# Attention with expert layers: batch 0 walked by halves of the sequence, its expert layers run as two groups of 256 tokens

## The chip, the cores and the metric

The kernel runs on one core of a Trainium2 chip. The time is device microseconds of one execution. The kernel before took 851.01 us (median of three runs, 849.23 to 852.69).

A core has five engines with queues of their own: TensorE (PE in the profile, with PEld for its weight loads), VectorE (DVE), ScalarE (ACT), GpSimd (POOL) and SyncE (SP), which here issues all transfers. Each works through its own instructions in order, and semaphores hold an instruction until what it needs is there.

## The reference, cut to what matters

Windowed attention with global tokens, for 8 batches and 8 heads of width 64. Each batch has 512 local and 32 global tokens. A global query sees all 544 keys. A local query sees the 32 global keys and the local ones at most 32 positions away. The 544 tokens of a batch, with their 8 heads side by side (512 columns), then go through an expert layer:

```
h = np.maximum(np.maximum(x @ w1, x @ w2), x @ w3)      # [512, 768] each
out = h @ w_out                                         # [768, 512]
```

The weights come as 64-bit floats, the rest as 32-bit floats.

## The kernel before, in words

**Tiles and steps.** Heads are taken in pairs, four pairs to a batch, 32 pairs (p) in all. The queries of a pair are cut into four tiles (t) of 128, so there are 128 steps (`sl`, with p and t from `divmod(sl, 4)`), 16 to a batch. The main loop of `body` (L510) walks these steps. In step `sl` it transposes the probabilities of the next step (`trans`, L338), computes scores and softmax some steps ahead (`next_scores`, `scores`, L300), multiplies probabilities with values (`pv`, L377), takes a part of the next pair's global queries (`glob`, `glob_soft`), transposes a part of the global probabilities (`transg`, L360), and prepares and loads what later steps need.

**Precision.** The first 26 to 28 steps multiply in full 32-bit floats. Later steps, and all expert matmuls, work in the faster rounded format (F32R) with each operand split into a high and a low part (`copy`, then `sub`), three matmuls to a product (high by high, high by low, low by high).

**Probabilities.** For steps 0 to 15 (`EARLY`) `scores` leaves them where the transposition reads them (`early`, one of five buffers in turn). From step 16 on they go by a transfer from `s` to `prob` (L334), a transfer being the way in which a tile gets into the rounded format without a computing engine. The global probabilities are scaled as a whole by `times`, and six transfers (L298) put their parts where `transg` reads them (`probg`).

**The expert layer.** `moe_group` (L415) is a generator that gives out one matmul at a time. For each of 6 x 3 blocks of 128 hidden columns it has 12 matmuls (L425) into one PSUM bank; copies and maxima over w1, w2 and w3 follow, and the split of h. Then come 18 matmuls for each 128 tokens (L444) with the output weights. `fill(n)` takes n matmuls from the generator. In the main loop 4 + 4 + 3 + 7 = 18 of them stand between the parts of a step. Batch b's 288 matmuls so fill the 16 steps of batch b + 1. Batch 7's and the global tokens' come at the end. In steps 0 to 15 there is no expert work.

**Weights.** `pieces` gives 24 pieces of 128 x 512 (18 of w1, w2 and w3, then 6 of w_out). `convert` takes one through five stages: the load of the 64-bit numbers into a staging tile (L160), an absolute value on ScalarE (L165), four integer operations on VectorE that put a 32-bit float together (L168 to L171), the high part on ScalarE (L178), the low part on POOL (L182). `weight_step` moves every piece under way on by one stage, takes one more into work and loads another. The list `WS` (L472) gives the number of such steps after each attention step: 13 through step 15, 17 in steps 16 to 25. Staging uses tiles that the expert layer later needs for h (`h0` to `h5`, six at first, fewer as the pieces go on); the scratch tile `cut` has six buffers.

**What sets the order.** Where an operation may run on several engines, a planner at build time (`least`, L79) takes the engine on which its own sums, with assumed costs, come out lowest. The framework adds all semaphores and buffer waits. It orders the instructions of each engine, the program's order being the priority. An explicit edge (`issue_after`, L349) puts everything that TensorE gets after the transposition of step 16 behind that transposition.

## Time and profile before

| | |
|---|---|
| Median of three runs | 851.01 us |
| The profiled execution's own time | 852.36 us |
| Its span | 850.6 us |
| TensorE busy | 811.6 us (95%) |
| VectorE busy | 566.0 us (67%) |
| ScalarE busy | 527.9 us (62%) |
| POOL busy | 510.0 us (60%) |
| First expert matmul | 76.6 us from the start |
| First expert matmul of batch 1 | 194.2 us from the start |

The profile shows one execution. Busy time is a union over an engine's instructions, and the span is what lies between the first and the last of them. A row of a window view gives the stretch, then the busy time of PE, PEld, DVE, ACT and POOL in it, the TensorE clock that was granted (1 is full), the busy share of the transfer engines and the rate in GB/s. A row of a group gives line, engine, operation, output and inputs, the count, and behind the bar the busy time, the mean duration in ns and the idle time of the engine before those instructions with what ended it. A row of waits reads: who waited, on what, us in total, how often, the longest.

### The profile page before, as it was taken

What the parts mean: (1) busy time and instruction counts of PE and PEld (TensorE: products, weight loads), DVE (VectorE), ACT (ScalarE), POOL (GpSimd) and SP (SyncE); (2) the same over time, 40 slices, a digit from 0 to 9 for tenths busy, and PEclk for the clock granted to TensorE, in tenths of its full rate; (3) what the DMA queues carried; (4) which work ended last, traced back from release to release, by engine and by line L of the source; (5) the groups of instructions that cost most, each with busy time, mean ns of one, the idle gap of its engine ahead of it and who ended that gap; (6) DMA issues with size and microseconds to landing.
All of it is one profiled execution on the core that took longest, in us unless ns stands there. A gap on an engine that the chain in (4) does not pass through costs nothing.

```text
span 850.6 us, 15712 instructions
## 1 busy us (share of the span) xinstructions
PE 811.6 (95%) x4452; PEld 674.6 (79%) x4452; DVE 566.0 (67%) x1784; ACT 527.9 (62%) x1479; POOL 510.0 (60%) x683
## 2 busy tenths in 40 slices
PE   6767987999999999999999999999999999999997
PEld 4545666788888888888888888888888888888896
DVE  4768786776777777777777777867786776421111
ACT  5666556767767676766776777776776676411111
POOL 5645666786668666766768766866676664411211
PEclk9798989999999999999999999999999999999999
DMA  6655755434333533353333433253335322100000
GB/s 199 173 175 159 223 168 161 125 109 136 111 108 89 155 101 104 105 163 113 95 107 114 136 110 102 85 161 106 98 113 162 101 85 67 65 12 1 25 25 25
DMA packets 102886, 95.12 MB, mean 112 GB/s; under 512 B 20752, under 2 KB 93584, under 8 KB 102800
## 3 DMA queue, kind: packets, MB, share of 16 engines
q1 hardware_dynamic: 102800, 94.12, 36.3%
q8 instruction: 36, 0.59, 0.3%
q14 instruction: 50, 0.41, 0.2%
HBM read 56.85 MB, written 8.91 MB: 77 GB/s over the span
## 4 chain that ended last, share of the span: by engine, by line
PE 87%; DVE 5%; DMA 2%; issue 2%; ACT 2%; SPq 1%; POOL 0%; DVEq 0%; ACTq 0%; POOLq 0%
PE pm L425 48%; PE pm L444 17%; PE O L394 7%; PE S L322 5%; PE T L346 4%; PE S L277 2%; PE O L387 1%; DVE wraw L170 1%; DMA wraw<-w_in 1%; PE S L367 1%; PE pm L318 1%; PE S L318 1%; DVE cut L169 1%; DVE cut L168 1%; PE S L273 0%
## 5 line engine op out<-in xcount | busy, mean ns | idle before, releaser
L425 PE MATMUL pm<-xs,wh 128*128 128x512 f32 (+1 forms) x1296 | 409.4, 389 | 0.8 <-POOL xs L94 0.8
L425 PEld LDWEIGHTS pm<-xs,wh 128*128 128x128 f32 x1296 | 234.2, 190 | 32.8 <-POOL xs L94 1.2
L425 PE MATMUL pm<-xs,wl 128*128 128x512 f32 (+1 forms) x648 | 254.1, 392 | 0.0
L112 POOL TENSOR_SCALAR s<-s,z 128x192 f32<-128x192 f32 (+1 forms) x220 | 101.6, 474 | 67.0 <-ACT lox L102 36.5
L425 PEld LDWEIGHTS pm<-xs,wl 128*128 128x128 f32 x648 | 123.0, 190 | 23.5 <-issue 2.4
L444 PE MATMUL pm<-woh,h 128*128 128x512 f32 x408 | 133.4, 398 | 0.0
L94 POOL TENSOR_TENSOR h<-m,h 128x512 fp32r<-128x512 f32 (+1 forms) x54 | 67.9, 1258 | 99.6 <-ACT h L102 99.6
L433 DVE TENSOR_TENSOR m<-pm,m 128x512 f32<-128x512 f32 (+1 forms) x108 | 71.2, 659 | 72.6 <-PE pm L425 71.6
L327 ACT ACTIVATE s<-s,nm 128x192 f32<-128x192 f32 (+1 forms) x224 | 103.1, 461 | 9.1 <-DVE nm L325 6.9
L94 POOL TENSOR_TENSOR qs<-qraw,qs 128x256 fp32r<-128x256 f32 x100 | 73.9, 749 | 57.4 <-ACT qs L102 44.0
L94 DVE TENSOR_TENSOR pt<-T,pt 128x512 fp32r<-128x512 f32 x102 | 70.5, 691 | 46.4 <-ACT pt L102 44.7
L329 DVE TENSOR_SCALAR z<-z 128x2 f32<-128x2 f32 x128 | 54.9, 429 | 48.7 <-ACT s L327 47.6
L444 PEld LDWEIGHTS pm<-woh,h 128*128 128x128 f32 x408 | 74.6, 188 | 11.6
L325 DVE CUSTOM_DVE_ANT_0 s<-S,mask 128x192 f32<-128x192 f32 (+1 forms) x224 | 74.7, 371 | 12.0 <-PE S L318 5.5
L444 PE MATMUL pm<-wol,h 128*128 128x512 f32 x204 | 81.7, 401 | 0.0
L94 POOL TENSOR_TENSOR vs<-vraw,vs 128x256 fp32r<-128x256 f32 x102 | 75.2, 737 | 7.7 <-ACT vs L102 3.6
L94 POOL TENSOR_TENSOR kst<-kraw,kst 64x576 fp32r<-64x576 f32 x49 | 70.1, 1430 | 11.4 <-issue 6.9
L102 ACT CAST pt<-T 128x512 fp32r<-128x512 f32 x90 | 52.7, 586 | 38.3 <-PE T L346 38.3
L102 ACT CAST qs<-qraw 128x256 fp32r<-128x256 f32 x100 | 40.7, 407 | 56.1 <-PE S L322 55.1
L394 PEld LDWEIGHTS O<-pt,vs 128*128 128x128 f32 x408 | 66.4, 188 | 9.2
L394 PE MATMUL O<-pt,vs 128*128 128x320 f32 (+1 forms) x408 | 72.8, 299 | 0.0
L346 PEld LDWEIGHTS T<-identr,prob 128*128 128x128 f32 x448 | 50.8, 141 | 20.6 <-ACT xr L102 2.3
(100 smaller groups left out, 1312.4 us busy)
## 6 DMA issues: line engine op xcount, KB each, us to landing
vraw<-v_in SPq DMA_DIRECT2D x128, 128.0 KB, 2.3
qraw<-q_in SPq DMA_DIRECT2D x100, 128.0 KB, 2.2
prob<-s SPq DMA_DIRECT2D x56, 224.0 KB, 2.4
prob<-s SPq DMA_DIRECT2D x56, 192.0 KB, 2.3
wraw<-w_in SPq DMA_DIRECT2D x18, 512.0 KB, 4.8
out_dram<-o SPq DMA_DIRECT2D x32, 256.0 KB, 2.5
kraw<-k_in SPq DMA_DIRECT2D x25, 320.0 KB, 3.1
qn<-q_in SPq DMA_DIRECT2D x28, 128.0 KB, 2.8
```

Of the source, the lines that this page charges most:

```text
L94: (dve if least(c) == "d" else pool).tensor_tensor(out=out, in0=a, in1=b, op=ALU.subtract)
L102: act.copy(out=out, in_=a)
L112: pool.tensor_scalar(out=out, in0=a, scalar1=col, scalar2=1.0, op0=ALU.mult, op1=ALU.mult)
L322: pe.matmul(ph[j][:, 0:n], lhsT=qs[sl][:, a, 128 * j:128 * j + 128], rhs=kst[p][:, j, c0:c0 + n], start=(a == 0), stop=(a == 1))
L325: dve.tensor_tensor_reduce(out=s[:, j, 0:n], in0=ph[j][:, 0:n], in1=mask[:, (1, 0, 1, 0)[t], 32 * (t == 0):32 * (t == 0) + n], scale=-0.12 ...
L327: act.activation(out=s[:, j, 0:n], in_=s[:, j, 0:n], func=AF.Exp, bias=nm[:, j:j + 1], scale=-1.0, accum_out=z[:, j:j + 1])
L329: dve.tensor_scalar(out=z, in0=z, scalar1=1e-9, scalar2=None, op0=ALU.add)
L346: i = pe.transpose(pr[:, 256 * j + 128 * c:256 * j + 128 * c + 128], s[:, j, 128 * c:128 * c + 128], one)
L394: pe.matmul(o[:, j, 0:320].rearrange("p (a q) -> p a q", a=2)[:, :, 0:n], lhsT=vs[sl][:, 2 * j + c].rearrange("p a d -> p (a d)"), rhs=pt[ ...
L425: pe.matmul(ps[:, 0:n], lhsT=w[f][:, i, k], rhs=xs[k][:, a, 0:n], start=(q == 0), stop=(q == 11))
L433: dve.tensor_tensor(out=m[:, 0:n], in0=ps[:, 0:n], in1=m[:, 0:n], op=ALU.max)
L444: pe.matmul(ps, lhsT=hh[f][:, a, 128 * t:128 * t + 128], rhs=w[:, f], start=(q == 0), stop=(q == 17))
```

## The change

Four things change together, nearly all of them in the first 32 steps.

1. **Order.** `ORDER` makes the steps 0 to 7 of batch 0 take the first two tiles of all four pairs, and the steps 8 to 15 the last two. The first 256 tokens of batch 0 are then ready after step 7. Keys of the four pairs are loaded ahead (`load_k4`), q (for the first 16 steps) and v (throughout) two steps to a transfer. v now has two buffers of two steps where it had three of one.
2. **Expert layers of batch 0 by halves.** `moe_local(0, 0, 256)` starts at step 8, with 7 + 6 + 5 + 9 = 27 matmuls to a step; `moe_local(0, 256, 256)` is chained behind it at step 16, with 18 to a step as before. In a group of 256 tokens two blocks of h share one tile, so that it needs `h0` to `h2` alone. `split_x` writes half of each activation tile at a time. All other batches keep groups of 512.
3. **Weights.** They come packed in one array of 24 contiguous pieces. `WS` now has 12 weight steps in the steps 0 to 7, 16 in the steps 8 to 15 and 2 after them. Staging uses three buffers (`h3` to `h5`), and the scratch tile three (two that values need later, one of its own).
4. **Probabilities.** `s4` with four buffers takes the place of `early` and of the later `s`. For batch 0's pairs the global probabilities are scaled by six operations that write straight into `probg`, in place of one scaling and six transfers, and are transposed in full 32-bit floats. `prob` and `probg` are set to zero where they are first needed. The explicit edge behind the transposition of step 16 is gone.

The diff, cut to its core:

```diff
+ORDER = [4 * p + 2 * h + t for h in range(2) for p in range(4) for t in range(2)] + list(range(16, NS))
...
-    def STAGE(n):
-
-        return n % 6 if n < N3 else 3 + n % 3 if n < N2 else 4 + n % 2 if n < N1 else 5
-
-    N3, N2, N1 = 12, 19, 22
...
-        src, k, m, dh, dl = piece
-        n, i = 512, STAGE(m)
-        r = moe.tile([128, n], mybir.dt.int64, name="wraw", tag=f"h{i}")
-        nc.sync.dma_start(out=r.rearrange("p (k f) -> p k f", k=k) if k > 1 else r, in_=src)
+        m, dh, dl = piece
+        r = moe.tile([128, 512], mybir.dt.int64, name="wraw", tag=f"h{3 + m % 3}")
+        nc.sync.dma_start(out=r, in_=win[m])
...
-        c = cut[:, m % 6] if m < 18 else moe.tile([128, n], I32, name="wct", bufs=3)
+        c = att.tile([128, 512], I32, name="wct", tag="vs") if m % 3 < 2 else moe.tile([128, 512], I32, name="wct")
...
     def load_v(s):
-        if s < NS:
-            vraw[s] = att.tile([128, 4, D], F32, name="vraw", bufs=3)
-            nc.sync.dma_start(out=vraw[s], in_=vin[s].rearrange("p (x d) -> p x d", d=D))
+        if s < NS and s % 2 == 0:
+            t = att.tile([128, 2, 4, D], F32, name="vraw")
+            nc.sync.dma_start(out=t, in_=vin[ORDER[s]:ORDER[s] + 2].rearrange("n p (x d) -> p n x d", d=D))
+            vraw[s], vraw[s + 1] = t[:, 0], t[:, 1]
...
+        pgt[p] = g = const.tile([128, 3, 128], F32 if p < NP else F32R, name="probg",
+                                tag=f"prob{p % 4}" if p < NP else f"prob{p % 2}")
+        if p < NP + 2:
+            pool.memset(g if p < NP else f32(g), 0.0)
+        if p < NP:
+            for c0, n, i, h, d0 in GPUT:
+                times(g[64 * h:64 * h + 64, i, d0:d0 + n], s[:, c0:c0 + n], z[:, 0:1], move=h == 1)
+            return
...
-        if sl == EARLY:
-
-            ctx.enter_context(tc.issue_after(i.ins))
...
-            ht = moe.tile([128, 2, 512], F32R, name=f"h{f}", tag=f"h{f}")
+            if n == 512:
+                ht = moe.tile([128, 2, 512], F32R, name=f"h{f}", tag=f"h{f}")
+            else:
+                if f % 2 == 0:
+                    two.append(moe.tile([128, 2, 2, 256], F32R, name=f"h{f // 2}", tag=f"h{f // 2}"))
+                ht = two[-1][:, f % 2]
...
-    WS = [0, 0, 0, 1, 0, 1, 0, 1, 0, 1, 0, 1, 2, 2, 1, 2, 2, 1, 2, 2, 1, 2, 2, 1, 2, 2]
+    WS = [1, 1, 2, 1, 2, 2, 1, 2] + [2] * 8 + [1] * 2
...
-        if sl % 16 == 0 and b:
-            fill(400)
-            mm[0] = moe_local(b - 1)
+        if sl == 8:
+            mm[0] = moe_local(0, 0, 256)
+        elif sl == 16:
+            mm[0] = chain(mm[0], moe_local(0, 256, 256))
+        elif sl >= 32 and sl % 16 == 0:
+            fill(400)
+            mm[0] = moe_local(b - 1)
+        n = (7, 6, 5, 9) if sl < 16 else (4, 4, 3, 7)
...
+        if sl < 8:
+            if t == 1:
+                xs.setdefault(0, []).append(split_x(xr[p][:, 0:2, 0:128]))
+        elif sl < 16:
+            if t == 3:
+                split_x(xr[p][:, 2:4, 0:128], xs[0][p], 256)
+        elif sl % 16 >= 12:
+            q = b * NP + sl % 16 - 12
+            xs.setdefault(b, []).append(split_x(xr[q][:, :, 0:128]))
```

More of the change, by code (lines that the diff above doesn't have):

```diff
@@ L1 @@
 from contextlib import ExitStack
+from itertools import chain
 import numpy as np
@@ L102, in copy, with times @@
             act.copy(out=out, in_=a)
-    def times(out, a, col):
+    def times(out, a, col, move=False):
         n = width(out)
-        e = least({"d": n * 0.52 + 125, "a": n * 0.833 + 185, "p": n * 1.27 + 150})
+        c = {"d": n * 0.52 + 125, "a": n * 0.833 + 185}
+        if not move:
+            c["p"] = n * 1.27 + 150
+        e = least(c)
         if e == "d":
@@ L173, in convert @@
         yield
-        if m >= 18:
-            if not wo:
-                wo.extend(const.tile([128, 6, DM], F32R, name=t, tag=t) for t in ("woh", "wol"))
-            dh, dl = [w[:, dh] for w in wo]
         act.copy(out=dh, in_=f32(c))
@@ L205, in weight_step, with load_k4, nat_k @@
         weight_load()
-    NS = 4 * B * NP
     NAT = 26
-    EARLY, AHEAD = 16, 9
-    kraw, kst, qraw, qs, vraw, vs, xr, sc, pg, pts = [{} for _ in range(10)]
+    EARLY = 16
+    kraw, kst, qraw, qs, vraw, vs, xr, sc, pg, pts, pgt = [{} for _ in range(11)]
+    prob = []
+    kn, qg = [], []
+    def load_k4(i):
+        if i == 0:
+            kn.extend(att.tile([128, 2, KW], F32, name="kn", tag="kst") for _ in range(2))
+            qg.append(att.tile([128, NP, 2 * SG], F32, name="qg", tag="kraw", bufs=1))
+            nc.sync.dma_start(out=kn[0][:, 0], in_=kin[0][:, 0:KW])
+            nc.sync.dma_start(out=qg[0], in_=kin[0:NP, :, KW:].rearrange("n p g -> p n g"))
+        elif i == 1:
+            nc.sync.dma_start(out=kn[0][:, 1], in_=kin[1][:, 0:KW])
+        else:
+            nc.sync.dma_start(out=kn[1], in_=kin[2:4, :, 0:KW].rearrange("n p g -> p n g"))
+    def nat_k(p):
+        if p < NP:
+            return kn[p // 2][:, p % 2], qg[0][:, p]
+        return kraw[p][:, 0:KW], kraw[p][:, KW:]
     def load_k(p):
@@ L271, in glob @@
         if 4 * p in NATK:
-            pe.matmul(ps[0:64, 0:n], lhsT=kraw[p][:, KW:KW + 2 * SG], rhs=kraw[p][:, c0:c0 + n], start=True, stop=True)
+            k, g = nat_k(p)
+            pe.matmul(ps[0:64, 0:n], lhsT=g, rhs=k[:, c0:c0 + n], start=True, stop=True)
             in1 = zero[0:64].to_broadcast([64, n])
@@ L332, in scores @@
             times(s[:, j, 0:n], s[:, j, 0:n], z[:, j:j + 1])
-        if sl >= EARLY:
-            nc.sync.dma_start(out=f32(sc[sl])[:, :, 0:n], in_=s[:, :, 0:n])
+        if i >= EARLY:
+            nc.sync.dma_start(out=f32(sc[i])[:, :, 0:n], in_=s[:, :, 0:n])
         spend("d", 2 * (n * 1.04 + 220) + 440)
@@ L405, in pv, with split_x @@
                               axis=AX.X, op=ALU.add)
-    def split_x(src, n):
-        t = xp.tile([128, 2, SL], F32R, name="xs")
-        d = [t[:, a, 0:n].rearrange("p (x q) -> p x q", x=src.shape[1]) for a in range(2)]
+    def split_x(src, t=None, c0=0):
+        n = src.shape[1] * src.shape[2]
+        if t is None:
+            t = xp.tile([128, 2, SL], F32R, name="xs")
+        d = [t[:, a, c0:c0 + n].rearrange("p (x q) -> p x q", x=src.shape[1]) for a in range(2)]
         copy(d[0], src)
@@ L486, in next_scores @@
             ahead[0] += 1
-    load_k(0)
+    load_k4(0)
     load_q(0)
-    mraw = cut[:, 5, 0:448].bitcast(F32)
-    nc.sync.dma_start(out=mraw, in_=min_.rearrange("p t c -> p (t c)"))
-    dve.tensor_copy(out=mask[:, :, 0:224], in_=mraw.rearrange("p (t c) -> p t c", t=2))
-    load_q(1)
+    mraw = moe.tile([128, 2, 224], F32, name="mraw", tag="h3")
+    nc.sync.dma_start(out=mraw, in_=min_)
+    dve.tensor_copy(out=mask[:, :, 0:224], in_=mraw)
+    load_v(0)
+    load_k4(1)
     load_q(2)
-    load_v(0)
-    load_k(1)
-    load_q(3)
     next_scores(1)
```

162 lines of the change are left out of this document (91 added, 71 removed).

## The prediction

> **What bounds the kernel now.** First the page: span, busy shares, slices.
>
> ```profile
> span 850.6 us, 15712 instructions
> ...
> PE 811.6 (95%) x4452; PEld 674.6 (79%) x4452; DVE 566.0 (67%) x1784; ACT 527.9 (62%) x1479; POOL 510.0 (60%) x683
> ...
> PE   6767987999999999999999999999999999999997
> ```
>
> TensorE is the bound nearly everywhere; its idle time (850.6 - 811.6 = 39 us) lies in the first seven or eight slices. So I cut the span where the kernel's stages end, with each engine's busy time (columns: PE, PEld, DVE, ACT, POOL, granted clock, DMA share, GB/s), and looked up in the timeline where batch 1's expert matmuls (L425) begin.
>
> ```profile
> 0.00:13.20 13.20, 9.27 (x32) 6.68 (x33) 5.41 (x35) 4.92 (x15) 5.42 (x14) 1.00 0.57 177
> 13.20:76.60 63.40, 45.82 (x278) 31.43 (x276) 45.03 (x157) 44.57 (x139) 36.27 (x50) 0.84 0.62 185
> 76.60:158.50 81.90, 69.14 (x361) 51.75 (x360) 63.90 (x153) 49.39 (x131) 54.17 (x53) 0.94 0.54 168
> 158.50:194.30 35.80, 35.80 (x200) 30.13 (x199) 27.85 (x91) 25.36 (x74) 26.40 (x38) 1.00 0.45 132
> ...
> 194.30:790.00 595.70, 595.70 (x3241) 504.23 (x3241) 415.01 (x1331) 394.82 (x1105) 379.08 (x521) 1.00 0.34 102
> 790.00:850.60 60.60, 55.86 (x349) 50.35 (x347) 8.75 (x19) 8.85 (x19) 8.62 (x12) 0.99 0.08 27
> ```
>
> ```profile
> 194.19 0.70 PE L425 MATMUL pm<-xs,wh 128*128 128x512 f32 x2
> ```
>
> Up to 76.6 us the kernel does batch 0's attention (loop steps 0 to 15) and no expert matmul. From 76.6 to 194.3 it does batch 1's attention (steps 16 to 31) with batch 0's experts between; at 194.2 batch 1's experts begin. From 194.3 to 790 TensorE has no idle time, and the diff leaves that work as it is. So the whole question is **when step 32 starts**, now at 194.3 us. Call part 1 the time up to step 16 and part 2 the time from 16 to 32. In part 1 TensorE works 55.1 of 76.6 us and VectorE 50.4; in part 2, 104.9 and 91.8 of 117.7.
>
> **What half-width groups cost TensorE.** Two places of the dense tail give the pitch:
>
> ```profile
> 784.85 0.39 PE L425 MATMUL pm<-xs,wl 128*128 128x512 f32 x1
> ...
> 785.53 0.39 PE L425 MATMUL pm<-xs,wl 128*128 128x512 f32 x1
> ...
> 811.83 0.28 PE L425 MATMUL pm<-xs,wl 128*128 128x256 f32 x1
> ...
> 812.19 0.28 PE L425 MATMUL pm<-xs,wl 128*128 128x256 f32 x1
> ```
>
> Three matmuls lie between each two rows: 0.227 us each with 512 columns, 0.120 with 256. Batch 0's 216 matmuls of L425 become 432: 51.8 instead of 49.0 us, +2.8. The 72 output matmuls (L444) stay 512 wide: 16.3 us. So nothing is saved; work moves. Steps 8 to 15 take 27 expert matmuls each, the first 216 (25.9 us). Steps 16 to 31 keep 18 each: 36 L444, 216 half-width L425, 36 L444, that is 42.3 us in place of 288 x 0.227 = 65.4.
>
> **Part 1, the weights.** All 24 weight conversions must now be through by step 16 instead of step 25. Each is four VectorE operations (L168 to L171). Their busy time up to 76.6 us, and the sum up to 194.3, in line order:
>
> ```profile
> 0.00:76.60 76.60, 5.35 (x10) 0.87 0.61 184
> ...
> sum 194.30, DVE 14.88; mean DVE 7.44
> ...
> 0.00:76.60 76.60, 6.41 (x10) 0.87 0.61 184
> ...
> sum 194.30, DVE 15.36; mean DVE 7.68
> ...
> 0.00:76.60 76.60, 7.93 (x10) 0.87 0.61 184
> ...
> sum 194.30, DVE 21.72; mean DVE 10.86
> ...
> 0.00:76.60 76.60, 7.21 (x9) 0.87 0.61 184
> ...
> sum 194.30, DVE 18.09; mean DVE 9.05
> ```
>
> ```profile
> L433 DVE TENSOR_TENSOR m<-pm,m 128x256 f32<-128x256 f32 x12 | 5.1, 425 | 19.3 <-PE pm L425 19.3
> ```
>
> 24 pieces take 70.1 us, 2.92 each. Part 1 now holds 26.9 of it, so its other VectorE work is 50.4 - 26.9 = 23.5. Added is one half group's maxima, 5.1 us by the row of the 256-wide group. New part 1 on VectorE: 23.5 + 70.1 + 5.1 = 98.7 us; TensorE gets 55.1 + 25.9 = 81. VectorE becomes the bound there. The first 13.2 us start up as now and hold 5.4 of it, so 93.3 us remain, at some utilisation. The low end is the crowded row 76.6:158.5, 63.9/81.9 = 0.78; the high end is 1. The fullest single stretches are these:
>
> ```profile
> 70.00:80.00 10.00, 6.79 (x45) 5.16 (x45) 9.25 (x27) 6.49 (x17) 4.81 (x7) 0.95 0.50 145
> 100.00:110.00 10.00, 5.80 (x33) 4.21 (x31) 9.93 (x17) 5.76 (x16) 7.87 (x8) 0.93 0.59 196
> ```
>
> I take their mean, 0.96, because the new part 1 has no transfer between probabilities and transpose, which the crowded stretch waits for. 93.3/0.96 = 97.2; step 16 would start at **110.4 us** (106.5 to 132.8).
>
> **Part 2.** TensorE's attention there is 104.9 - 65.4 = 39.5 us, at a mean granted clock of about 0.96 (0.94 and 1.00 above, by length); at full clock 37.9. With 42.3 for the experts that is 80.2. VectorE falls to 91.8 - 43.2 (its pieces) = about 49, so TensorE is the bound, and what it still waits for is this:
>
> ```profile
> PE S L367 <- DMA probg<-sg: 4.5, 1, 4.5
> ```
>
> Both transfers stay from step 16 on, with fewer weight loads ahead of them on SP; I keep 2 us of the 4.5 (0 to twice that, since the probabilities' own transfer to the transpose has fewer matmuls to hide behind in steps of some 5 us). Part 2 is **82.2 us** (80.2 to 89.2).
>
> **Edits costed at nothing.** For batch 0's pairs the six scatter transfers per pair become six multiplications by ScalarE, VectorE or POOL; at most 24 operations on half the partitions, hidden under VectorE's work unless VectorE gets them: bound 0 to 24 x 0.41 (the undisturbed wide L168 row further below) = 10 us. The kernel's planner gives work to the least loaded engine, which is not VectorE here, so I take 0. Fp32 transposes of the global probabilities and the later memsets lie under VectorE's work. Paired and contiguous loads take work from SP, which bounds nothing. Dropping the ordering edge behind the transpose of step 16 only lets TensorE start earlier. The h tiles of a half fit three buffers, which leaves the other three as weight staging.
>
> **Sum.** 110.4 + 82.2 = 192.6 against 194.3: -1.7 us on the profiled execution's own 852.36 (span 850.6 and 1.76 around it), so 850.7. The median of the runs, 851.01, stands 1.35 below that execution: **849 us**. The forecast is that the work is only exchanged: part 1 grows by 34, part 2 shrinks by 35. Its own range, by 0.93 to 1 in part 1 and the bounds of part 2, is 843 to 857.
>
> **Rival one, faster: the VectorE work is less than its busy time.** In this stretch the same operations last twice as long while POOL runs a subtraction:
>
> ```profile
> 59.19 1.44 DVE L169 TENSOR_SCALAR cut<-cut 128x512 int32<-128x512 int32 x1
> 60.66 1.78 DVE L170 SCALAR_TENSOR_TENSOR wraw<-wraw,cut 128x512 int32<-128x512 int32 x1
> 62.37 0.41 DVE L168 TENSOR_SCALAR cut<-cut 128x512 f32<-128x512 f32 x1
> 62.70 0.68 DVE L171 SCALAR_TENSOR_TENSOR cut<-wraw 128x512 int32<-128x512 int32 x1
> 63.31 0.41 DVE L169 TENSOR_SCALAR cut<-cut 128x512 int32<-128x512 int32 x1
> 63.75 0.69 DVE L170 SCALAR_TENSOR_TENSOR wraw<-wraw,cut 128x512 int32<-128x512 int32 x1
> ```
>
> ```profile
> 59.07 1.28 POOL L182 TENSOR_TENSOR wl<-cut,wh 128x512 fp32r<-128x512 f32 x1 [0.36 <-ACT wh L178]
> 60.63 1.26 POOL L94 TENSOR_TENSOR xs<-xr,xs 128x512 fp32r<-128x512 f32 x1 [0.29 <-ACT xs L102]
> ```
>
> Undisturbed a piece costs 2.19 us, 0.73 less. If the new order lets them miss each other, 24 x 0.73/0.96 = 18 us go: **831 us**; half of that, 840. For it: TensorE's 34 us of idle time before 194.3 bound the gain, and 18 lies inside. Against it: each piece brings its own POOL subtraction, now 24 in part 1 instead of 9. The Trainium skill's page SBUF — State Buffer, Who interferes with whom, says that a VectorE instruction with two SBUF inputs or in a two-port mode and a GpSimd instruction hold one port pair exclusively, the later one blocking in full. The overlaps at 59 and 60.6 us agree; by that rule the stretching comes with every piece, which speaks for the 2.92.
>
> **Rival two, slower: the conversion ring.** Staging shrinks from six buffers to three and the scratch tile from six to three, so a piece's load waits for the VectorE work of the piece three before, and its first ScalarE operation (L165) for that piece's POOL subtraction. Behind a waiting L165 on ScalarE stand the exponentials and the copies of transposed probabilities, for which TensorE's next product waits. On SP the load also stands behind the paired v load, which with two pair buffers waits in even steps for the next step's product on TensorE.
>
> ```profile
> wraw<-w_in SPq DMA_DIRECT2D x18, 512.0 KB, 4.8
> ...
> wraw<-wo_in SPq DMA_DIRECT2D x6, 512.0 KB, 3.8
> ```
>
> ```profile
> L182 POOL TENSOR_TENSOR wl<-cut,wh 128x512 fp32r<-128x512 f32 x18 | 25.1, 1398 | 15.0 <-ACT wh L178 15.0
> ...
> L165 ACT ACTIVATE cut<-wraw 128x512 f32<-128x512 f32 x18 | 12.1, 675 | 6.6 <-DMA wraw<-w_in 6.3 <-POOL xs L94 0.3
> ```
>
> ```profile
> 19.67 0.65 ACT L165 ACTIVATE cut<-wraw 128x512 f32<-128x512 f32 x1
> ```
>
> ```profile
> SPq L253 <- PE O L387: 7.6, 5, 2.0
> ```
>
> One turn, three pieces: 3.8 to 4.8 + 0.68 + 2.92 + 1.40 + 2.0 = 10.8 to 11.8 us, 3.6 to 3.9 a piece. From 19.7 us, 24 pieces end at 106 to 113, and two steps of 27 x 0.12 + 45.8/16 = 6.1 us follow: 118 to 125 in place of 110.4, so **857 to 864 us**. It decides once a turn exceeds the time in which VectorE and the attention work take three pieces, 3 x 97.2/24 = 12 us with all of part 1's work in it. For it: the loads already are what ScalarE waits for here, and the turn is within 1 us of that pace. Against it: a turn spans one and a half steps of some 7 us, so the load mostly hides.
>
> **Rival three.** The first half's matmuls start at step 8 but stand in TensorE's order behind late pieces, and the second half's last reads at step 29 hold back batch 1's activations from step 28, so the exchange gives nothing: 852 to 855.
>
> **How the numbers follow.** Forecast 0.38, rival one 0.32, rival two 0.25, rival three 0.05. The range leaves out the ends of both rivals: **833 to 863**. With 0.5% (4.3 us) as what can be told from no change, the forecast's own range leans 0.07 to faster and 0.04 to slower: faster 0.32 + 0.07 = 0.39; slower 0.25 + 0.04 = 0.29; the same, 0.32.
>
> **What would show it.** Batch 1's first 512-wide expert matmul at about 192 to 193 us; the first 256-wide output matmuls at 108 to 113; VectorE 95% busy before that and below 65% after; L168 to L171 still near 70 us. The forecast is wrong if those four fall to 55 (rival one), or if ScalarE's L165 waits for transfers or POOL by over 10 us in sum (rival two).

## The result, and the profile after

The changed kernel takes 859.1 us (median of four runs, 857.71 to 860.29), the kernel before took 850.12 in the same series (848.09 to 852.69). The ratio is 1.0103, with an interval of 1.007 to 1.0137: slower by about 9 us, where 849 and no change were forecast. The profiled execution after took 859.45 us, 7.1 more than the one before.

The page after, in the rows that answer to those shown of before:

```profile
span 857.4 us, 15953 instructions
...
PE 814.9 (95%) x4668; PEld 688.3 (80%) x4668; DVE 573.7 (67%) x1806; ACT 530.8 (62%) x1497; POOL 517.2 (60%) x705
...
PE   6668779989999999999999999999999999999997
...
DVE  5889964587778677777777777867787776511111
```

TensorE's busy time grew by 3.3 us (811.6 to 814.9), its idle time by 3.5 (39.0 to 42.5). The loss lies in the first quarter again, so the timeline gives the same two marks as before: the first output matmul of the first half (the end of part 1) and batch 1's first expert matmul (the end of part 2).

```profile
118.69 0.73 PE L470 MATMUL pm<-woh,h 128*128 128x512 f32 x2 [0.39 <-ACT m L105]
...
200.88 0.70 PE L451 MATMUL pm<-xs,wh 128*128 128x512 f32 x2
```

Step 32 starts at 200.9 us where it was 194.3, 6.7 later, and that is nearly all of the 6.8 us by which the span grew. The windows, cut at these marks (PE, PEld, DVE, ACT, POOL, granted clock, DMA share, GB/s), say which part it is:

```profile
0.00:13.20 13.20, 7.99 (x29) 5.88 (x29) 4.84 (x31) 6.11 (x18) 5.49 (x16) 1.00 0.88 286
13.20:60.00 46.80, 32.53 (x177) 21.88 (x176) 38.11 (x113) 31.65 (x95) 29.09 (x41) 0.78 0.52 166
60.00:110.00 50.00, 38.55 (x281) 32.83 (x279) 48.80 (x101) 31.97 (x84) 38.80 (x38) 0.93 0.53 174
110.00:118.70 8.70, 6.91 (x43) 6.23 (x43) 7.92 (x23) 4.42 (x12) 5.41 (x7) 0.80 0.41 130
...
118.70:200.90 82.20, 77.14 (x558) 66.93 (x558) 47.55 (x189) 53.85 (x168) 51.77 (x78) 1.00 0.42 125
200.90:797.00 596.10, 596.10 (x3243) 504.35 (x3242) 417.75 (x1332) 394.03 (x1106) 378.10 (x520) 1.00 0.34 103
```

Part 2 lasts 82.2 us, the number of the forecast. Part 1 lasts 118.7 instead of 110.4. VectorE does 99.67 us of work in it (98.7 forecast), so the sum of the work is right; but it is idle for 8.7 of the 46.8 us between 13.2 and 60 us (0.81 busy), while from 60 to 110 it is 0.98 busy. Its waits in the first of these stretches (who waited, on what, us, times, longest), and TensorE's up to 195 us:

```profile
DVE s L346 <- PE S L339: 3.3, 3, 2.3
DVE sg L291 <- PE S L283: 3.2, 5, 1.9
DVE s L346 <- PE pm L339: 1.2, 2, 0.9
```

```profile
PE S L385 <- DMA wraw<-w_in: 6.2, 1, 6.2
PE pm L451 <- DVE m L459: 5.5, 3, 4.0
PE T L367 <- DMA prob<-s: 4.4, 3, 3.6
```

VectorE waits there for products of scores, which TensorE has not reached, and TensorE waits for what others still owe it. The longest of its waits, 6.24 us, ends at 52.76 us; the row names a transfer of weights, but the transposition (L385) reads global probabilities, the row of the weight load for the same line names POOL, and the timeline of POOL has their scaling (L118) just before, behind a subtraction of a weight piece (L166):

```profile
PEld S L385 <- POOL probg L118: 8.0, 2, 6.5
...
50.49 1.43 POOL L166 TENSOR_TENSOR wl<-wct,wh 128x512 fp32r<-128x512 f32 x1
51.90 1.12 POOL L118 TENSOR_SCALAR probg<-sg,zg 64x128 f32<-64x128 f32 x2
```

That POOL was the true releaser is read from these rows; a run further below tests it.

A second long wait stands near the end of part 1. Step 16 is the first whose probabilities go by a transfer, and their transposition comes in step 15, before the first output matmul:

```profile
111.41 0.58 PE L367 MATMUL T<-identr,prob 128*128 128x128 f32 x4 [3.64 <-DMA prob<-s]
...
105.34 1.70 POOL L166 TENSOR_TENSOR wol<-wct,woh 128x512 fp32r<-128x512 f32 x1 [1.28 <-ACT woh L163]
107.03 1.79 POOL L118 TENSOR_SCALAR s<-s,z 128x192 f32<-128x192 f32 x2
```

TensorE does nothing from 107.8 to 111.4 us. The transfer is issued at 108.84, when POOL's scaling of these probabilities has ended, and that scaling again began right behind a weight subtraction. VectorE is busy all through this wait, so the rows do not tell how much of it part 1 would lose with an earlier transfer.

The conversions themselves (groups of VectorE up to 118.7 us; behind the bar busy time, mean ns, idle before):

```profile
L160 DVE SCALAR_TENSOR_TENSOR wct<-wraw 128x512 int32<-128x512 int32 x24 | 23.7, 988 | 0.0
L159 DVE SCALAR_TENSOR_TENSOR wraw<-wraw,wct 128x512 int32<-128x512 int32 x24 | 22.8, 948 | 0.3 <-DVE nm L346 0.2
L157 DVE TENSOR_SCALAR wct<-wct 128x512 f32<-128x512 f32 x24 | 14.3, 595 | 2.0 <-ACT wct L154 2.0
L158 DVE TENSOR_SCALAR wct<-wct 128x512 int32<-128x512 int32 x24 | 13.9, 580 | 0.2
```

Together 74.7 us, 3.11 a piece (2.92 forecast), and VectorE waits only 2.0 us for the stage ahead of it. The loads in turn wait for VectorE (waits of SyncE's queue up to 118.7 us):

```profile
SPq L149 <- DVE wct L160: 19.5, 6, 5.0
SPq L149 <- DVE wct L157: 16.9, 7, 6.2
SPq L149 <- DVE wct L158: 14.1, 3, 5.2
```

### The profile page after: what moved, and what is told of

It is laid out like the page before. It is cut to its first block, busy times and chain, and to the rows that moved or that the text cites. A ratio compares the mean times of both kernels' runs of the same rounds, so it can differ in the third digit from the quotient of the medians.

```text
span 857.4 us, 15953 instructions
## 1 busy us (share of the span) xinstructions
PE 814.9 (95%) x4668; PEld 688.3 (80%) x4668; DVE 573.7 (67%) x1806; ACT 530.8 (62%) x1497; POOL 517.2 (60%) x705
## 4 chain that ended last, share of the span: by engine, by line
PE 86%; DVE 7%; DMA 2%; issue 2%; ACT 1%; POOL 1%; SPq 0%; POOLq 0%; DVEq 0%; ACTq 0%
PE pm L451 48%; PE pm L470 16%; PE O L412 6%; PE S L343 5%; PE T L367 4%; PE S L287 2%; PE O L405 1%; DVE wct L160 1%; DVE wraw L159 1%; PE S L339 1%; DVE wct L157 1%; PE S L385 1%; PE S L283 1%; DVE z L350 1%; DVE s L346 1%
## 5 line engine op out<-in xcount | busy, mean ns | idle before, releaser
L451 PE MATMUL pm<-xs,wh 128*128 128x512 f32 (+1 forms) x1440 | 424.6, 370 | 8.8 <-DVE m L459 5.5
L451 PEld LDWEIGHTS pm<-xs,wh 128*128 128x128 f32 x1440 | 255.5, 191 | 40.4 <-DVE m L459 6.2
L451 PE MATMUL pm<-xs,wl 128*128 128x512 f32 (+1 forms) x720 | 266.6, 370 | 4.3 <-POOL wl L166 4.3
L118 POOL TENSOR_SCALAR s<-s,z 128x224 f32<-128x224 f32 (+1 forms) x248 | 114.7, 475 | 82.7 <-ACT lox L105 36.0
L451 PEld LDWEIGHTS pm<-xs,wl 128*128 128x128 f32 x720 | 137.4, 191 | 26.1 <-POOL wl L166 4.7
L97 POOL TENSOR_TENSOR h<-m,h 128x512 fp32r<-128x512 f32 (+1 forms) x60 | 70.7, 1178 | 98.6 <-ACT h L105 98.5
L348 ACT ACTIVATE s<-s,nm 128x224 f32<-128x224 f32 (+1 forms) x256 | 118.2, 462 | 17.5 <-DVE nm L346 13.5
L346 DVE CUSTOM_DVE_ANT_0 s<-S,mask 128x224 f32<-128x224 f32 (+1 forms) x240 | 80.6, 370 | 23.3 <-PE S L339 17.7
L470 PEld LDWEIGHTS pm<-woh,h 128*128 128x128 f32 x408 | 74.6, 188 | 13.9 <-POOL h L97 1.7
L343 PEld LDWEIGHTS S<-kst,qs 128*128 128x128 f32 x400 | 59.3, 190 | 9.4 <-DVE nmg L291 1.1
```

The costliest lines, as they stand in the source:

```text
L97: (dve if least(c) == "d" else pool).tensor_tensor(out=out, in0=a, in1=b, op=ALU.subtract)
L118: pool.tensor_scalar(out=out, in0=a, scalar1=col, scalar2=1.0, op0=ALU.mult, op1=ALU.mult)
L343: pe.matmul(ph[j][:, 0:n], lhsT=qs[i][:, a, 128 * j:128 * j + 128], rhs=kst[p][:, j, c0:c0 + n], start=(a == 0), stop=(a == 1))
L346: dve.tensor_tensor_reduce(out=s[:, j, 0:n], in0=ph[j][:, 0:n], in1=mask[:, (1, 0, 1, 0)[t], 32 * (t == 0):32 * (t == 0) + n], scale=-0.12 ...
L348: act.activation(out=s[:, j, 0:n], in_=s[:, j, 0:n], func=AF.Exp, bias=nm[:, j:j + 1], scale=-1.0, accum_out=z[:, j:j + 1])
L451: pe.matmul(ps[:, 0:n], lhsT=w[f][:, i, k], rhs=xs[k][:, a, c0:c0 + n], start=(q == 0), stop=(q == 11))
```

## The experiments

The first question was whether VectorE's work sets the end of part 1; then whether the order of TensorE's work does; then which part of the change costs what; and last where the gain comes from that one of these runs brought to light. Ratios are to the kernel before, run on the same chip (its medians there are 850.7 to 851.9 us); 0.1% is 0.85 us. Runs on different chips are best compared by their ratios. The three runs that leave out part of a weight's conversion have one execution each and no interval. Edits are against the changed kernel unless said otherwise.

### VectorE's share of part 1

The first run leaves out two of the four integer operations:

```diff
-        dve.tensor_scalar(out=f32(c), in0=f32(c), scalar1=2.0 ** -15, scalar2=HIMAX, op0=ALU.max, op1=ALU.min)
-        dve.tensor_scalar(out=c, in0=c, scalar1=0x07FFFFFF, scalar2=3, op0=ALU.bitwise_and, op1=ALU.logical_shift_left)
```

> The changed kernel with two of the four VectorE operations of every weight conversion left out (the clamp and the shift of the upper word), so its weights are not the reference's. In the changed kernel these two take 14.3 + 13.9 = 28 us of VectorE before the first output matmul at 118.7 us. If VectorE's work is what sets part 1 (theory), the first output matmul comes some 20 to 28 us earlier, until TensorE's 78 us or ScalarE take over, and the span falls from 857 to about 832 to 838. If the staging ring or TensorE's order sets it (rival), the first output matmul moves by less than 8 us.

849.0 us. The two groups taken out had 28.2 us of VectorE; the first output matmul moves from 118.69 to 108.20, 10.5 earlier, between the two expectations. So VectorE is on the path, but only for a third of what was taken away: VectorE then waits 11.2 us for ScalarE's absolute values.

The second leaves VectorE's instructions and puts a ScalarE copy in the place of POOL's subtraction:

```diff
-        pool.tensor_tensor(out=dl, in0=f32(c), in1=f32(dh), op=ALU.subtract)
-        spend("p", 1350)
+        act.copy(out=dl, in_=f32(c))
```

> The changed kernel with the POOL subtraction of every weight conversion replaced by a ScalarE copy of the whole value, so the low parts of the weights are not the reference's. POOL loses 35 us before 118.7 us, ScalarE gains about 15. If VectorE's operations are stretched by POOL's subtractions (part of the theory), L157 to L160 fall from 74.7 us towards 24 x 2.19 = 53 us and the span falls by 10 to 20 us. If they are not, they stay above 70 us and the span stays within 3 us of 857.

845.7 us. The same four groups, up to 118.7 us:

```profile
L160 DVE SCALAR_TENSOR_TENSOR wct<-wraw 128x512 int32<-128x512 int32 x24 | 17.2, 716 | 0.1
L159 DVE SCALAR_TENSOR_TENSOR wraw<-wraw,wct 128x512 int32<-128x512 int32 x24 | 16.8, 700 | 0.5 <-DVE nm L345 0.2
L157 DVE TENSOR_SCALAR wct<-wct 128x512 f32<-128x512 f32 x24 | 12.9, 535 | 3.8 <-ACT wct L154 3.7
L158 DVE TENSOR_SCALAR wct<-wct 128x512 int32<-128x512 int32 x24 | 11.3, 471 | 0.3
```

58.1 us instead of 74.7: 16.6 us of VectorE's busy time are the price of POOL's subtractions beside it. Part 1 ends at 104.80, 13.9 earlier. The kernel before gains too with the same edit (its L182), but less:

> The kernel before, with the POOL subtraction of every weight conversion replaced by a ScalarE copy of the whole value, so the low parts of the weights are not the reference's. In the changed kernel this edit took 13.4 us. Theory: before, VectorE is busy 142 of 194 us and no stretch is full for long, so the shorter operations give less, 3 to 7 us (843 to 848). Rival (the port waits bound both kernels alike): 12 to 15 us, 835 to 839.

847.3 us, 4.6 less than the kernel before on that chip (851.89).

The work can't simply be dropped, so the subtraction was moved to VectorE itself:

```diff
-        pool.tensor_tensor(out=dl, in0=f32(c), in1=f32(dh), op=ALU.subtract)
-        spend("p", 1350)
+        dve.tensor_tensor(out=dl, in0=f32(c), in1=f32(dh), op=ALU.subtract)
+        spend("d", 650)
```

> The changed kernel with the low part's subtraction on VectorE in place of POOL, same values. VectorE gets 24 x 0.69 = 16.6 us of work and loses the waits that those subtractions cause, 74.7 - 58.1 = 16.6 us. Theory: the two cancel, the time stays within 4 us of 859, though POOL loses 35 us of its work before the first output matmul. Rival (it is POOL's place in the chain, not VectorE's time, that costs): 846 to 852.

858.4 us, ratio 1.0069 [1.0049, 1.0089]. The four operations fall to 57.1 us and the subtraction adds 17.4: what VectorE is spared in waiting, it pays in work.

### The order of TensorE's work

In the changed kernel the first expert matmul already runs at 27.7 us, since the edge that kept TensorE's order is gone. The first rival was that these early matmuls block attention:

```diff
-                pe.transpose(pr[:, 256 * j + 128 * c:256 * j + 128 * c + 128], s[:, j, 128 * c:128 * c + 128], one)
+                i = pe.transpose(pr[:, 256 * j + 128 * c:256 * j + 128 * c + 128], s[:, j, 128 * c:128 * c + 128], one)
+        if sl == 9:
+            ctx.enter_context(tc.issue_after(i.ins))
```

> The changed kernel with an ordering edge put back: everything that TensorE gets after the transposition emitted in step 8 stays behind it, so that no expert matmul goes ahead of its step (in the changed kernel the first stands at 27.7 us, and TensorE waits 8 us in all for POOL's low parts and activations before 70 us). Theory (VectorE sets part 1): the span moves by less than 3 us either way. Rival (early expert matmuls block TensorE and through it VectorE, which is idle 8.7 of the 46.8 us from 13.2 to 60): the span falls by 5 to 8 us, to about 850.

859.3 us, ratio 1.0096 [1.0069, 1.0123]: no change that can be told; part 1 ends at 117.5. The first expert matmul now runs at 57.8 us, and TensorE's waits for pieces of weights up to the end of part 1 (4.3 us in the changed kernel) are gone. So early expert matmuls, or their waiting for late pieces, are not what costs the time, which speaks against rival three's first half.

The second idea was to need the weights later by doing all output matmuls of both halves at the end. For it `moe_group` is split into `moe_in` and `moe_out`, and the second half's h lies in the other three tiles, with the staging fitted to that; the diff is cut to the order and the pace:

```diff
-            mm[0] = moe_local(0, 0, 256)
+            mm[0] = moe_in(xs[0], 0, 256, ha)
         elif sl == 16:
-            mm[0] = chain(mm[0], moe_local(0, 256, 256))
+            mm[0] = chain(mm[0], moe_in(xs[0], 256, 256, hb, 3),
+                          moe_out(ha, 256, local_out(0, 0)), moe_out(hb, 256, local_out(0, 256)))
...
-    WS = [1, 1, 2, 1, 2, 2, 1, 2] + [2] * 8 + [1] * 2
+    WS = [1, 2, 1, 1, 2, 1, 2, 2, 1, 1, 2, 1, 1, 2, 1] + [1] * 6
```

> The changed kernel with the output matmuls of both halves moved behind the second half's L451 block, so that the six pieces of w_out are first needed at step 28; the weight steps are spread, 21 by step 14 and 6 more in steps 15 to 20; the second half's h lies in the other three tiles. Theory: 6 x 3.1 = 19 us of VectorE's work go from part 1, where VectorE is full, to part 2, where it is busy 47.5 of 82 us; batch 1's first expert matmul comes at 180 to 187 us instead of 200.9, and the time is 840 to 846 us, less than the 850 of before. Rival (the conversion chain's latency, not VectorE's work, sets part 1): within 4 us of the changed kernel's 859.

854.9 us, ratio 1.0047 [1.0031, 1.0064]. A gain of 4, not the 13 to 19 expected. VectorE is full from 70 to 110 us (9.86 to 9.96 of each 10 us) and still 0.82 and 0.90 busy in the next two stretches of 10 us; these rows fit that only the point moves at which TensorE meets it, and no run tests that. With the subtraction on VectorE besides (as above), and the first 16 steps' scaling kept off POOL:

```diff
-            times(s[:, j, 0:n], s[:, j, 0:n], z[:, j:j + 1])
+            times(s[:, j, 0:n], s[:, j, 0:n], z[:, j:j + 1], move=i < EARLY)
```

> The kernel with the output matmuls moved behind both halves and spread weight steps, with in addition the low part's subtraction on VectorE and the scaling of the probabilities of the first 16 steps kept off POOL, same values as the reference. VectorE then runs nearly without POOL beside it in part 1: its pieces should take 24 x (2.2 + 0.6) = 67 us in place of 75, and the time should come to 846 to 852 us in place of 855. Within 2 us of 855 if the waits come from elsewhere.

849.0 us, ratio 0.9969 [0.9951, 0.9987], as expected, and still above what follows.

### The parts of the change by themselves

Now the expert layers' halves and the early weights were taken out, and all else was kept: one group of 512 tokens from step 16, the weights in the staging of before, and nearly at its pace (13 weight steps through step 15, where the list of before adds up to 12, not 13). The scratch tile keeps three buffers.

```diff
-        r = moe.tile([128, 512], mybir.dt.int64, name="wraw", tag=f"h{3 + m % 3}")
+        r = moe.tile([128, 512], mybir.dt.int64, name="wraw", tag=f"h{m % 6 if m < 12 else 3 + m % 3 if m < 19 else 4 + m % 2 if m < 22 else 5}")
...
-    WS = [1, 1, 2, 1, 2, 2, 1, 2] + [2] * 8 + [1] * 2
+    WS = [0, 0, 0, 1, 0, 1, 0, 1, 0, 1, 0, 1] + [2] * 11
...
-        if sl == 8:
-            mm[0] = moe_local(0, 0, 256)
-        elif sl == 16:
-            mm[0] = chain(mm[0], moe_local(0, 256, 256))
+        if sl == 16:
+            mm[0] = moe_local(0)
```

> The changed kernel with batch 0's experts as one group of 512 tokens from step 16 on, and with the weight steps late again (6 through step 11, then 2 a step to step 22); the walk by halves, the packed weights, the paired loads and the direct scaling of the global probabilities stay. Theory (the loss is the weights' VectorE work drawn into part 1): the time goes back to about that of before, 848 to 854 us, and batch 1's first expert matmul to 192 to 197. Rival (one of the other edits costs it): 856 to 862.

**844.4 us, ratio 0.991 [0.9881, 0.9939]: faster than both kernels.** Neither expectation had this. Step 16's probabilities are transposed at 68.2 us (74.7 before), and batch 1's experts begin at 186.5:

```profile
68.23 0.53 PE L367 MATMUL T<-identr,prob 128*128 128x128 f32 x4 [1.59 <-DMA prob<-s]
...
13.20:60.00 46.80, 39.00 (x256) 26.51 (x255) 40.10 (x150) 37.01 (x119) 32.30 (x55) 0.93 0.67 221
60.00:120.00 60.00, 49.54 (x263) 35.72 (x262) 57.59 (x125) 38.91 (x104) 48.21 (x42) 0.97 0.49 159
```

VectorE is about as busy up to 120 us as in the changed kernel, with 75.2 us for the same conversions. TensorE gets 39.0 of the 46.8 us instead of 32.5.

From here the edits are against this version. First the early pace and the three staging buffers put back, still with one group:

```diff
-        r = moe.tile([128, 512], mybir.dt.int64, name="wraw", tag=f"h{m % 6 if m < 12 else 3 + m % 3 if m < 19 else 4 + m % 2 if m < 22 else 5}")
+        r = moe.tile([128, 512], mybir.dt.int64, name="wraw", tag=f"h{3 + m % 3}")
...
-    WS = [0, 0, 0, 1, 0, 1, 0, 1, 0, 1, 0, 1] + [2] * 11
+    WS = [1, 1, 2, 1, 2, 2, 1, 2] + [2] * 8 + [1] * 2
```

> The kernel with one group of 512 tokens from step 16, with the changed kernel's early weight steps (28 through step 15) and its three staging buffers; no expert matmul before step 16 in the program. Theory: the loss comes with the early weights, since VectorE's 75 us of conversion then fill part 1 while part 2 has TensorE's full 105 us: 858 to 866 us, worse than or like the changed kernel, with VectorE over 90% busy from 20 us to step 16. Rival (early weights are free, the early halves cost): 843 to 848.

858.4 us, ratio 1.0087 [1.0072, 1.0102]. Early weights, with the shorter staging that belongs to them, bring nearly the whole loss; starting the halves' expert work at step 8 besides (the changed kernel, 859.1) wins nothing back that can be told.

```profile
13.20:60.00 46.80, 32.06 (x169) 19.95 (x168) 43.45 (x122) 34.14 (x104) 31.43 (x43) 0.74 0.56 192
60.00:120.00 60.00, 44.99 (x228) 30.96 (x226) 59.11 (x131) 38.90 (x108) 46.69 (x47) 0.83 0.50 164
120.00:160.00 40.00, 38.87 (x220) 30.25 (x221) 16.93 (x61) 20.49 (x60) 20.00 (x28) 1.00 0.36 111
```

VectorE is full (43.45 + 59.11 of 106.8 us, 0.96) and TensorE has 77.1 us of work there instead of 88.5. Step 16's probabilities come at 95.5 us, 27 later. How VectorE's time is shared out shows why: between 13.2 and 60 us the four conversion operations take 33.1 of its 43.45 us and leave 10.3 for the softmax and the rest. With late weights they take 18.2 of 40.10 and leave 21.9. In the changed kernel it is 27.4 of 38.11, which leaves 10.7. So the softmax stands behind conversions there. After 120 us VectorE has little to do (16.93 of 40) and TensorE runs without gaps, but what it lost is gone.

Only the three staging buffers, at the late pace:

```diff
-        r = moe.tile([128, 512], mybir.dt.int64, name="wraw", tag=f"h{m % 6 if m < 12 else 3 + m % 3 if m < 19 else 4 + m % 2 if m < 22 else 5}")
+        r = moe.tile([128, 512], mybir.dt.int64, name="wraw", tag=f"h{3 + m % 3 if m < 19 else 4 + m % 2 if m < 22 else 5}")
```

> One group of 512 with late weights (844.4), but three staging buffers from the first piece on, as in the changed kernel. Theory (the short ring bounds nothing; the 14 us of the early weights came from VectorE's work moving ahead of batch 0's attention): 843 to 847. Rival two of the prediction (the ring holds the loads back): 850 to 858.

848.7 us, ratio 0.9969 [0.9953, 0.9985], between the two expectations. The ring costs about 0.6%, 5 us, which leaves 10 of the 15 us for the pace, if the two add.

Only the halves, both from step 16 on, at the late pace:

```diff
-            mm[0] = moe_local(0)
+            mm[0] = chain(moe_local(0, 0, 256), moe_local(0, 256, 256))
...
-        n = (7, 6, 5, 9) if sl < 16 else (4, 4, 3, 7)
+        n = (8, 7, 6, 11) if 16 <= sl < 32 else (4, 4, 3, 7)
```

> The kernel with one group from step 16 (844.4 us), with batch 0's experts as two groups of 256 tokens again, but both from step 16 on, 32 matmuls to a step; weight steps late as there. Halving adds 2.8 us of TensorE work and a second pass of maxima. Theory (the loss came from the weights' VectorE work in part 1, not from the halves): 845 to 850 us. Rival (256-wide groups themselves cost, by waits at each block's end): 854 to 860.

854.9 us, ratio 1.0048 [1.003, 1.0066]: about 1.4%, 12 us, for 2.8 us of matmul time. The first output matmul comes at 125.3 us instead of 163.3, and TensorE now waits for pieces of w_out (2.9 us) and for the probabilities of steps that come in quicker turn:

```profile
PE T L367 <- DMA prob<-s: 8.9, 4, 5.2
...
PE pm L470 <- POOL wol L166: 2.9, 3, 1.3
```

With the output matmuls of both halves put last, so that w_out is needed as late as with one group, and again with the second half's h in the other three tiles (the split of `moe_group` is left out of the diff):

```diff
-            mm[0] = chain(moe_local(0, 0, 256), moe_local(0, 256, 256))
+            mm[0] = chain(moe_in(xs[0], 0, 256, ha), moe_in(xs[0], 256, 256, hb, 3),
+                          moe_out(ha, 256, local_out(0, 0)), moe_out(hb, 256, local_out(0, 256)))
```

> Two groups of 256 tokens from step 16 on with the weights late, as before, but the output matmuls of both halves behind all of the expert-input matmuls, so that w_out is needed as late as with one group of 512. Theory (half-width groups in themselves cost little, 2.8 us by their matmuls; the 10 us of the late halves came from needing w_out early): 844 to 849 us. Rival (256-wide groups cost it anyway, through twice the maxima, copies and PSUM turns): 852 to 857.

850.4 us, ratio 0.9984 [0.997, 0.9999]: again between the two. Needing w_out early is about 5 of the 12 us, together with the reuse of the h tiles, which this edit takes away as well. Of the 6 left, 2.8 are the matmuls' own; the wait for the probabilities stays (9.2 us in four waits, against 5.1 in three with one group).

### Where the gain comes from

The ordering edge taken out of the kernel before:

```diff
-        if sl == EARLY:
-
-            ctx.enter_context(tc.issue_after(i.ins))
```

> The kernel before without the ordering edge behind the transposition of step 16. The kernel with one group from step 16 has its first expert matmul at 52 us in place of 76.6 and is 7.5 us faster than before. If the missing edge is what gives that, this run takes 842 to 847 us; if it is the direct scaling of the global probabilities and the loads, it stays at 849 to 853.

849.6 us, ratio 0.9979 [0.9967, 0.9991]: the edge is worth 2 us there, where the version with one group gains 7.5. Then, in the version with one group, batch 0's global probabilities scaled as a whole and moved by six transfers, as before:

```diff
+            times(s, s, z[:, 0:1])
             for c0, n, i, h, d0 in GPUT:
-                times(g[64 * h:64 * h + 64, i, d0:d0 + n], s[:, c0:c0 + n], z[:, 0:1], move=h == 1)
+                nc.sync.dma_start(out=g[64 * h:64 * h + 64, i, d0:d0 + n], in_=s[:, c0:c0 + n])
```

> One group of 512 with late weights (844.4), but the global probabilities of batch 0's pairs again scaled as a whole and moved by six transfers. Theory (the direct scaling is part of the gain that was costed at nothing, because TensorE's transposition waits less): 846 to 849. Rival (no part of it: the scaling is hidden as the prediction took it): 843 to 845.5.

851.9 us, ratio 1.0006 [0.9991, 1.0021], above both expectations, and the whole gain is gone: in this order of steps, with one group and late weights, the direct scaling is worth about 1%, 8 us. The waits and the window show how:

```profile
PE S L386 <- DMA probg<-sg: 10.8, 3, 4.0
...
13.20:60.00 46.80, 25.57 (x129) 16.45 (x127) 38.20 (x106) 26.66 (x74) 27.27 (x34) 0.72 0.57 193
```

With the direct scaling, up to the same 195 us:

```profile
PE S L385 <- DVE probg L114: 3.5, 2, 2.6
PE S L385 <- DMA probg<-sg: 1.8, 2, 1.4
```

TensorE waits 10.8 us for these transfers (1.8 with the scaling, which in its place makes it wait 3.5 for VectorE's multiplications and 1.2 for POOL's) and gets 25.6 us of work between 13.2 and 60 instead of 39.0. Whether the scaling alone would bring as much in the order of before was not tried: there the global probabilities of a pair are wanted every four steps, not every two.

The packed weights, undone:

```diff
-        nc.sync.dma_start(out=r, in_=win[m])
+        if m < 18:
+            f, i = divmod(m, 3)
+            nc.sync.dma_start(out=r.rearrange("p (k f) -> p k f", k=4),
+                              in_=(w1, w2, w3)[i][:, f * 128:(f + 1) * 128].rearrange("(k p) f -> p k f", p=128))
+        else:
+            nc.sync.dma_start(out=r, in_=w4[(m - 18) * 128:(m - 17) * 128])
...
```

> One group of 512 with late weights (844.4), but w1, w2, w3 and w_out loaded from their own four arrays as before. Theory (transfers of weights bound nothing, VectorE does): 843 to 846. Rival (the packed pieces land sooner and are the gain of 5 us): 848 to 851.

844.8 us, ratio 0.9925 [0.9902, 0.9948], not to be told from 0.991: the packing brings nothing.

The subtraction on VectorE in the version with one group, with the scaling of the first 16 steps kept off POOL (both as above), which was to beat it:

> The kernel with one group from step 16, with the low part's subtraction on VectorE and the scaling of the first 16 steps' probabilities kept off POOL, same values as the reference. The same two edits took 5.8 us from the kernel with the output matmuls moved back, where VectorE was full for longer. Here VectorE is above 90% busy from 20 to 120 us: 838 to 843 us if that stretch sets the end, 843 to 847 if it doesn't.

852.8 us, ratio 1.0014 [1.0, 1.0029], a miss. VectorE now waits for ScalarE on the softmax:

```profile
DVE z L350 <- ACT s L348: 12.7, 9, 4.0
```

That is its wait for the exponentials up to 160 us; with the subtraction on POOL it is 2.6. Two edits changed together here: ScalarE also got 14 scalings of the softmax in this time where it had 3. Which of the two costs the 8 us was not separated.

Last, the suspicion from the result: POOL's part of the global probabilities' scaling (12 of 24 operations, 4.7 us) given to ScalarE and VectorE, first in the changed kernel, then in the version with one group.

```diff
-                times(g[64 * h:64 * h + 64, i, d0:d0 + n], s[:, c0:c0 + n], z[:, 0:1], move=h == 1)
+                times(g[64 * h:64 * h + 64, i, d0:d0 + n], s[:, c0:c0 + n], z[:, 0:1], move=True)
```

> The changed kernel (859.1), but none of the 24 scalings of batch 0's global probabilities may go to POOL (12 did, 4.7 us). Theory (TensorE's early waits, of which the longest is 6.2 us, come from these scalings standing behind POOL's subtractions of weights): 850 to 855 us, part 1 ending at 110 to 115. Rival (these waits are covered by VectorE's work, which fills part 1 in any case): 857 to 861, part 1 ending at 117 to 120.

857.6 us, ratio 1.007 [1.0045, 1.0095]: inside the rival's range, and not to be told from the changed kernel's 1.0103. The wait of 6.2 us is gone, as it must be if POOL was its releaser. VectorE is busy 39.79 of the 46.8 us (38.11), but new waits take the place, the longest of them these:

```profile
PE pm L451 <- POOL xs L97: 4.3, 3, 3.0
...
PE T L367 <- DMA prob<-s: 3.8, 1, 3.8
PE S L385 <- DVE nm L346: 3.1, 1, 3.1
PE S L385 <- ACT probg L116: 2.8, 1, 2.8
```

Part 1 ends at 116.1, between the two expectations and 2.6 earlier of the 8.3 that were missed.

> One group of 512 with late weights (844.4), and none of the 24 scalings of batch 0's global probabilities on POOL (12 were there, 4.3 us). Theory (less waiting behind POOL's subtractions, TensorE waits 1.2 us for POOL there): 841 to 844. Rival (the scalings then stand on VectorE and ScalarE, which feed the softmax): 845 to 849.

**842.4 us, ratio 0.9891 [0.9863, 0.9919]**, the fastest of all and as the theory expected, though its interval overlaps that of 0.991.

## Why the prediction was wrong, and where it was right

**Part 2: the number right, by two misses that cancel.** "Part 2 is 82.2 us"; 82.2 were measured. TensorE worked 77.1 of them, where 80.2 were summed, and was idle for 5.1, where 2 were allowed. That TensorE is nearly full there, and that VectorE falls below 65% (47.55 of 82.2, 58%), held; that both misses are 3.1 us is luck.

**The failing step: the utilisation in part 1.** "I take their mean, 0.96 ... 93.3/0.96 = 97.2; step 16 would start at 110.4 us." The work came out as summed (99.67 us against 98.7), though its parts did not: the conversions took 74.7 instead of 70.1 and the rest 25.0 instead of 28.6. It took 105.5 us of time and not 97.2: 94.83/105.5 = 0.90. The two stretches from which 0.96 came are 10 us each, cut out where VectorE happened to be full; the prediction stretched them over 93 us. The row of the crowded stretch, 0.78 over 82 us, was the longer evidence, and 0.90 lies between. The reason given for leaving it aside, that the new part 1 "has no transfer between probabilities and transpose", fails at its end: step 16's transposition is in it, and TensorE stands still for 3.64 us until that transfer lands. Had the mean of 0.78 and 0.96 been taken (0.87), part 1 would have been 120.4. VectorE's idle time lies early, where it waits for score products of a TensorE that itself waits. From 60 us to the end of part 1 it is 0.97 busy (56.72 of 58.7 us), as forecast. The version with early weights and one group reached 0.96 from 13 to 120 us; there all of the experts are left for part 2, so its 858.4 us does not test this step. Counting one engine's busy time through a stretch in which two engines feed each other gives a bound from below, not a time.

**"The work is only exchanged": wrong.** The forecast had "part 1 grows by 34, part 2 shrinks by 35"; it was 42 and 35.5. The sum treated weights as movable from part 2 to part 1 at their own price. In part 2 of the kernel before, VectorE's conversions lay beside TensorE's expert work; in part 1 they share VectorE with the softmax that feeds TensorE. The pace costs about 10 us, the shorter ring 5 (858.4 for both with one group, 848.7 for the ring, 844.4 for neither), if the two add. The Trainium skill (Perfetto Trace Analysis, Optimization Strategy) says that interleaving stretches with different most-contended engines may improve performance; here the kernel that interleaves batch 0's attention with its expert matmuls, and needs its weights early for that, takes 859.1 us against 850.1.

**"Edits costed at nothing": wrong by about 8 us, on the other side of the bound.** The direct scaling was given 0 to 10 us of loss. It is a gain, 8 us in this order of steps, as measured in the version with one group; in the changed kernel it was not taken out by itself. The row that held it was in the trace of before and was not used. TensorE's waits up to 76.6 us have:

```profile
PE S L367 <- DMA probg<-sg: 6.8, 4, 3.0
```

The packed loads and the dropped edge were rightly small (none, and 2 us in the kernel before). So two errors of opposite sign stood in the sum: about 8 gained by the scaling and the rest, about 16 lost by halves with early weights and short staging (1.0103 against 0.991), 9 in all.

**What half-width groups cost: priced by their columns alone.** "+2.8" stands for the matmuls. With late weights the halves cost 12, of which about 5 go when the output matmuls are put last; on the last 3 us nothing was shown. With early weights, halves begun at step 8 and one group begun at step 16 take the same time (859.1 and 858.4), so nothing shows that this term made the forecast miss.

**Rival one (waits between VectorE and POOL): the mechanism is real, the hoped-for miss did not happen.** A piece took 3.11 us, not 2.19. Taking POOL's subtraction away gave 58.1 us, 2.42 a piece. That the stretching "speaks for the 2.92" was the right reading. The rule of the Trainium skill (SBUF — State Buffer, Who interferes with whom) agrees with these 16.6 us.

**Rival two (the conversion ring): its number, 857 to 864, holds the result, but its mechanism is the smaller part.** Its sign, ScalarE's absolute values waiting for transfers or POOL by over 10 us, is absent. ScalarE's waits up to 118.7 us have this one row for it:

```profile
ACT wct L154 <- DMA wraw<-w_in: 0.7, 1, 0.7
```

The loads do wait for VectorE, as the rival has it, but they still land before ScalarE wants them. The run with the ring alone gives it 5 us at the late pace; at the early pace ring and pace were not taken apart.

**Rival three: not borne out in its first half.** With the edge TensorE has no wait for weight pieces in part 1, and the time stays (859.3). Its second half, that the second half's last reads hold back batch 1's activations, was not tested by itself.

**The signs.** Batch 1's first expert matmul came at 200.9 us (192 to 193 expected) and the first output matmul at 118.69 (108 to 113). VectorE was 0.90 busy before it from 13.2 us on (95%) and 58% after it (below 65%). The four operations took 74.7 us (near 70), so neither sign of a rival, a fall to 55 or ScalarE waiting, appeared.

**What remains open.** The scaling on POOL behind the weights' subtractions is 2.6 of the 8.3 us by which part 1 is longer than summed, by one trace each. Why VectorE is idle for 8.7 us between 13.2 and 60 us is not settled beyond that: it waits for score products, and TensorE waits for VectorE, ScalarE and POOL in turn. The clock granted to TensorE is lower there as well (0.78, against 0.93 with one group and late weights), and how much of the loss that adds was not separated. That early pace and short ring cost 15 us together is measured, and the shares of VectorE's time show the softmax squeezed by conversions; that this alone makes the 15 us is argued.

## What to carry to other kernels

Work that fills an engine's gaps beside the bound is not free when it is moved ahead into a stretch where the same engine feeds the bound: look at which chain it will stand in front of, and take a utilisation from the longest stretch that resembles the new one, not from the fullest ten microseconds. When a change joins several edits, price the small ones from the waits that they take away, and try the change without its headline: here that version, with one group and late weights, takes 844.4 us (842.4 with the scaling off POOL), 0.9% less than the kernel before and 1.7% less than the change. Smaller groups can cost more than their matmul time (12 us here against 2.8, at late weights), since what they read is due earlier.

## What the runs showed of the hardware

In the changed kernel a VectorE operation beside several POOL operations lasts more than five times as long as alone (an undisturbed L159 takes 0.68 us):

```profile
35.72 3.85 DVE L159 SCALAR_TENSOR_TENSOR wraw<-wraw,wct 128x512 int32<-128x512 int32 x1
...
35.38 1.17 POOL L118 TENSOR_SCALAR probg<-sg,zg 64x128 f32<-64x128 f32 x3
36.52 2.49 POOL L166 TENSOR_TENSOR wl<-wct,wh 128x512 fp32r<-128x512 f32 x2
```

It began while the first POOL row ran (35.38 to 36.55 us) and ended at 39.57, 0.56 us after the second row did (39.01), so it lasted through the rest of these five POOL operations. TensorE waited 3.4 us, until 37.83, for a result of the same line L166. VectorE's busy time therefore holds waiting that no row of waits lists: 16.6 of the 74.7 us here go with POOL's subtractions. Moving the subtraction to VectorE gained nothing by itself (858.4 against 859.1). Together with scalings kept off POOL it gained in one version (849.0 against 854.9) and lost in another (852.8 against 844.4).
